# First chunk's weights and first x blocks packed by the host; T4's high part moved

## The chip, the cores and the metric

The kernel runs on one core of a Trainium2 chip. The metric is the device time of one execution in microseconds (us), as the median of several runs. A core has a matmul engine (PE, whose weight loads are listed apart as PEld), a vector engine (DVE), a scalar engine (ACT), GpSimd (POOL) and a sync engine (SP). Here SP issues all loads but a few, POOL issues the stores of intermediates, and 16 DMA engines carry them.

## The reference

An input x of 2048 rows (positions) by 512 columns goes through two branches, which a gate mixes. One branch is a Fourier mixing layer: real and imaginary products with 512 x 512 matrices, then with 2048 x 2048 matrices, real part only. The other is a gated feed-forward layer.

```python
a = x @ dft_hid_re.T
b = x @ dft_hid_im.T
y = dft_seq_re @ a - dft_seq_im @ b
h = silu(x @ w1) * (x @ w3)          # w1, w3: 512 x 1376
out = h @ w2                         # w2: 1376 x 512
g = sigmoid((x * gate_w).sum(-1, keepdims=True))
result = g * y + (1 - g) * out
```

All data are float32.

## The kernel before

Every float32 operand is split into a high part (a copy rounded to the type `F32R`, written by ACT: `high`, L108) and a low part (the source less its high part, a subtraction on DVE: `low`, L111). A product is three matmuls: high by high, and the two mixed ones (`mm3`, L119). One matmul has a 128 x 128 weight block and 512 moving columns.

On top of that, most products are done by a scheme of the Strassen kind: an operand is cut in a 2 x 2 arrangement of blocks, and seven products of sums of blocks replace eight. The blocks of x are called B11, B12, B21, B22, their sums T1 to T4 (`SUMS`, formed by `sum_xo`, L207, on DVE). The weights of w1 and w3 come in chunks of 128 columns; a chunk has four blocks, A11, A12, A22, A21, of 256 columns each, and sums of them (`sums_wb`, L246 to L249).

The program has an early stage, which makes silu(x w1) * (x w3) for all chunks and two groups of x (g = 0 and 1), and then a long stage of eight blocks for the sequence products and the product with w2. The change lies in the first forty microseconds of the early stage:

- Warm-up: DVE writes a bf16 tile of zeros, and `WARM` = 11 matmuls on it run while the first data come.
- Loads, all on the SP queue in the order in which they are written: A11 of chunk 0 (128 KB), B11 (512 KB), the other three blocks of chunk 0 (384 KB), B21, B12, B22 (512 KB each), then chunks 1 to 4 of the weights (512 KB each).
- Chunk 0 is done with the plain eight products: `half(i, j, w, x, start)` issues six matmuls into the bank C[i, j] (L428). The order is C00, C10 with B11, C00, C10 with B21, C01, C11 with B12, C01, C11 with B22. Each needs the splits that stand just before it in the program.
- Products of chunks 1 to 3 with B11 (`prod1`, bank X) and B21 (`prod2`, bank Y) follow, while ACT and DVE split the weights and make T1 to T4.
- From chunk 1 on, `gate_up(n)` does the other five products of a chunk, in the order X (T2), Z (T3), X of chunk n+3, X (T1), Z (T4), Y of chunk n+3, X (B22). Hooks named `early`, `second`, `mid` and `at_end` hold work of other parts that is to be written at set places in it. X is accumulated further after L373 has read it, and Z after ACT has copied it (L364).

The order on every engine is the written order (`manual_schedule`); an engine waits on semaphores for its operands. The places `F4` hold the raw x blocks: four of 512 KB, one for each block of the group, used again for the second group once the sums of the first are made. T2 is written over B11, T3 over B12 and T4 over B21.

Of the kernel before, what the change touches and what calls it, by code (L numbers as in the profile page):

```python
# [7 lines left out]
F32 = mybir.dt.float32  # L8
F32R = mybir.dt.float32r
# [3 lines left out]
P = 128  # L13
# [4 lines left out]
TB = 512  # L18
# [3 lines left out]
NG = NST // 2  # L22
NC = (F + P - 1) // P
NP2 = (NC + 1) // 2
WARM = 11
LOOK = 3
K = 9
W2_AT = (9, 11, 13, 15)
# [4 lines left out]
def fnet_swiglu_gate_kernel(  # L33
    ctx: ExitStack,
    tc: tile.TileContext,
    xn: bass.AP,
    xt: bass.AP,
    cc: bass.AP,
    dd: bass.AP,
    w13: bass.AP,  # L40
# [13 lines left out]
    nc = tc.nc  # L54

    def pool(name, bufs, side, space=None):
        kw = {} if space is None else {"space": space}
        cm = tc.tile_pool(name=name, bufs=bufs, side=side, reuse_waits="tile", **kw)
        return cm, cm.__enter__()
# [9 lines left out]
    xo0_cm, xo0 = pool("xo0", 1, "left")  # L69
    f4_a_cm, f4_a = pool("f4_a", 1, "right")  # L70
    wu_cm, wup = pool("wu", 1, "right")
    s1_cm, s1p = pool("s1", LOOK + 1, "right")
# [4 lines left out]
    xo1_cm, xo1 = pool("xo1", 1, "right")  # L77
# [18 lines left out]
    def wide(name):  # L96
        return take(F4, [P, 1024], F32, name)
# [9 lines left out]
    def high(hi, src):  # L107
        nc.scalar.activation(hi, src, AF.Copy)  # L108

    def low(hi, lo, src):  # L110
        nc.vector.tensor_sub(lo, src, hi.bitcast(F32))  # L111

    def split(hi, lo, src):
        high(hi, src)
        low(hi, lo, src)

    def mm3(ps, ah, al, bh, bl, first, last, chain=False):
        for n, (u, v) in enumerate(((ah, bh), (ah, bl), (al, bh))):
            nc.tensor.matmul(ps, u, v, start=first and n == 0, stop=last and n == 2,  # L119
                             skip_group_check=chain)  # L120
# [13 lines left out]
    def flat(ap):  # L134
        return ap.rearrange("p a n -> p (a n)")
# [53 lines left out]
    XO, ST = {}, {}  # L189
    XRAW = ("B12", "B11", "B21", "B22")  # L190

    def flat_x(ap):
        return ap.rearrange("p q n -> p (q n)")

    def load_xo(g, k):

        if g not in XO:
            XO[g] = (xo1 if g else xo0).tile([P, 2, 7, 2, 512], F32R, tag="xo", name=f"xo{g}")
        ST[g, k] = wide(f"xs{g}_{k}")
        nc.sync.dma_start(ST[g, k], xt[g, XRAW.index(k)])  # L200

    OPS = ("B11", "B21", "B22", "T1", "T2", "T3", "T4")
    SUMS = {"T1": ("B12", "B11"), "T2": ("B22", "T1"), "T3": ("B22", "B12"), "T4": ("B21", "T2")}

    def sum_xo(g, k, t):
        ST[g, k] = t
        nc.vector.tensor_sub(t, *(ST[g, v] for v in SUMS[k]))  # L207

    def xo_parts(g, k):
        o = XO[g][:, :, OPS.index(k)]  # L210
        return flat_x(o[:, 0]), flat_x(o[:, 1]), ST[g, k]

    def split_xo(g, k):
        split(*xo_parts(g, k))

    WS, WA, WB = {}, {}, {}

    def back(w):
        return w >= NC and SETS[w] > 0

    def load_w(w, lo=0, hi=4):
        if lo == 0:
            WS[w] = f4_a.tile([P, 4, 256], F32, tag=f"f4_{4 + w % (LOOK + 1)}", name=f"ws{w}")
        nc.sync.dma_start(WS[w][:, lo:hi].rearrange("p a n -> p (a n)"),
                          w13[SETS[w], :, lo * 256 : hi * 256])
# [7 lines left out]
    def wa_parts(w, lo, hi):  # L233
        return (*(flat(WA[w][:, h, lo:hi]) for h in range(2)), flat(WS[w][:, lo:hi]))

    def new_wa(w):

        WA[w] = wap.tile([P, 2, 3, 256], F32R, tag="wa", name=f"wa{w}")
# [24 lines left out]
    def prod(ps, n, wi, xi, start, chain=False):  # L263
        w = WSET[n]
        w, wi = (WA[w], wi) if wi < 3 else (WB[w], wi - 3)
        x = XO[ITEMS[n][1]]
        for q in range(2):
            sl = slice(q * P, (q + 1) * P)
            mm3(ps, w[:, 0, wi, sl], w[:, 1, wi, sl], x[:, 0, xi, q, :], x[:, 1, xi, q, :],
                start and q == 0, q == 1, chain)  # L270
# [51 lines left out]
    def store_h(n, k, h):  # L322

        c, g = ITEMS[n]
        j = min(c % (NP2 - 1) if c < NC - 1 else NP2 - 1, NP2 - 1)
        b = 2 * (NP2 - 1 <= c < NC - 1)
        nc.gpsimd.dma_start(hsp[g, b + k, j // 2, :, j % 2 * 512 : (j % 2 + 1) * 512], h)  # L327

    early, second, mid, at_end = {}, {}, {}, {}

    def run(work, n):
        for f in work.get(n, ()):
            f()

    def gate_up(n):
        last = NI - 1
        x, s1 = G.pop(n)
        z = bank(6 + n % 2, f"Z{n}")  # L340
        if n == last - 1:

            u2, g1 = (s1p.tile([P, 512], F32, tag="s1", name=f"{k}_{n}") for k in ("u2", "g1"))
        else:
            h = hp.tile([P, 1024], F32, tag="h", name=f"h{n}")
            u2, g1 = h[:, :512], h[:, 512:]
        u4 = u4p.tile([P, 512], F32, tag="u4", name=f"u4_{n}")
        nw = WSET[n + 1] if n < last else 0
        if nw in WB or nw == 0:
            nw = None  # L350
        elif back(nw):
            load_wb(nw)
            nw = None
        wa = WSET[n + LOOK + 1] if n + LOOK < last else 0
        if wa in WA or wa == 0:
            wa = None
        else:
            load_w(wa, 0, 3 if back(wa) else 4)

        prod(x, n, 4, 4, False, True)  # L360
        nc.scalar.activation(u2, x, AF.Copy)
        run(early, n)
        prod(z, n, 5, 5, True, True)
        nc.scalar.activation(u4, z, AF.Copy)  # L364
        run(second, n)
        if nw is not None:
            sums_wb(nw)
        if n + LOOK <= last:
            first1(n + LOOK)
        if nw is not None:  # L370
            high_wb(nw)
        prod(x, n, 3, 3, False, True)
        nc.vector.tensor_add(u4, u4, x)  # L373
        if nw is not None:
            low_wb(nw)
        run(mid, n)
        prod(z, n, 2, 6, False, True)
        nc.vector.tensor_add(u2, u2, z)
        nc.vector.tensor_mul(u2, s1, u2)  # L379
        store_h(n, 0, u2)  # L380
        if wa is not None:
            new_wa(wa)
            parts_a = wa_parts(wa, 0, 3)
            high(parts_a[0], parts_a[2])
        if n + LOOK <= last:
            first2(n + LOOK)
        if wa is not None:
            low(*parts_a)
        prod(x, n, 6, 2, False, True)
        nc.scalar.activation(g1, x, AF.Silu)  # L390
        put_score(n, 1, x)
        if n + LOOK <= last:
            gate1(n + LOOK)
        nc.vector.tensor_mul(g1, g1, u4)
        store_h(n, 1, g1)
        run(at_end, n)


    ctx.enter_context(tc.manual_schedule())
    load_w(0, 0, 1)  # L400
    load_xo(0, "B11")
    warm = s1p.tile([P, 1024], mybir.dt.bfloat16, tag="s1", name="warm")[:, :512]
    nc.vector.memset(warm, 0.0)  # L403
    wps = bank(7, "wps")
    for n in range(WARM):
        nc.tensor.matmul(wps, warm[:, :P], warm, start=True, stop=True)  # L406
    nc.scalar.activation(act0, warm[:, :24], AF.Silu)
    load_w(0, 1, 4)
    for k in ("B21", "B12", "B22"):
        load_xo(0, k)  # L410
    load_w(1)
    load_w(2)
# [4 lines left out]
    b12, a21 = zt[0].rearrange("p h a n -> p h (a n)"), zt[1][:, :, 0]  # L417
# [12 lines left out]

    def xo_half(k, q):
        i = OPS.index(k)
        return XO[0][:, 0, i, q], XO[0][:, 1, i, q], ST[0, k][:, q * 512 : (q + 1) * 512]

    s1 = s1p.tile([P, 512], F32, tag="s1", name="s1_0")
    g1 = u4p.tile([P, 512], F32, tag="u4", name="g1_0")
    h0 = hp.tile([P, 1024], F32, tag="h", name="h0")
    t1 = hp.tile([P, 1024], F32, tag="h", name="t1")
    new_wa(0)
    split(*wa_parts(0, 0, 1))  # L440

    hi, lo, src = xo_half("B11", 0)
    high(hi[:, :256], src[:, :256])
    nc.vector.tensor_copy(hi[:, 256:], src[:, 256:])
    low(hi, lo, src)
    split(*xo_half("B11", 1))
    half(0, 0, 0, 0, True)
    split(a21[:, 0], a21[:, 1], WS[0][:, 3])
    half(1, 0, None, 0, True)
    split(*wa_parts(0, 1, 3))  # L450
    for q in range(2):
        split(*xo_half("B21", q))
    half(0, 0, 1, 1, False)
    split(b12[:, 0], b12[:, 1], ST[0, "B12"])
    half(1, 0, 2, 1, False)
    split_xo(0, "B22")
    nc.scalar.activation(s1, C[0, 0], AF.Silu)
    half(0, 1, 0, None, True)
    WS.pop(0)
    load_w(4)  # L460
    sum_xo(0, "T1", t1)
    half(1, 1, None, None, True)
    nc.vector.tensor_mul(h0[:, :512], s1, C[1, 0])
    store_h(0, 0, h0[:, :512])
    sum_xo(0, "T2", ST[0, "B11"])
    half(0, 1, 1, 2, False)
    for w in (1, 2):
        new_wa(w)
        split(*wa_parts(w, 0, 3))
    half(1, 1, 2, 2, False)  # L470
    free(*zt)
    split_xo(0, "T2")
# [28 lines left out]
    def do(work, n, f, *a):  # L501
        work.setdefault(n, []).append(lambda: f(*a))


    do(early, 1, lambda: low(*xo_parts(0, "T1")))
    do(second, 1, lambda: split_xo(0, "T4"))
    do(second, 1, free, *(ST[0, b] for b in ("B11", "B21", "B12", "B22")))
    do(second, 1, sum_g, 2, y2)
    do(mid, 1, gate1, 2)
    do(early, 2, sum_g, 3, y3)  # L510
# [65 lines left out]
    for n in range(NI):  # L576
        if n in W2_AT:
            p = W2_AT.index(n)
# [4 lines left out]
        if n in A1_AT:  # L583
            p = A1_AT.index(n)
# [9 lines left out]
    n = NI - 1 - LOOK  # L594
# [332 lines left out]
    for i, (src, sp, p) in enumerate(late):  # L927
        blk, b = 1 + i // 2, i % 2
        n = (17, 24)[b]
# [11 lines left out]
    for p in range(KD):  # L941
        early = p < NG - NP2
# [71 lines left out]
```

## Time and profile before

| | before |
|---|---|
| median of 3 runs | 710.58 us (710.43 to 710.71) |
| profiled execution | 710.56 us |
| its span in the trace | 708.8 us |
| PE busy | 703.8 us (99%) |
| DVE busy | 605.4 us (85%) |
| ACT busy | 369.1 us (52%) |
| POOL busy | 64.0 us (9%) |
| HBM read, written | 114.82 MB, 57.16 MB |

The span runs from the first instruction of the program to the last. Busy time is the time in which an engine had an instruction in it; matmuls overlap one another in the pipeline, so the pace of PE is seen from the starts of groups of matmuls and not from their durations. In the timeline a row has the start, the duration, the engine, the line, the operation, the tiles (out <- in), the shape and a count, and in brackets the idle time before it and what ended it. A row with a count merges instructions that follow each other. PEclk is the granted PE clock.

### The profile page before, as it was taken

Reading aid. Unit: us, or ns where it says so; the run is one execution under the profiler, and the core shown is the slowest. Engines: PE = TensorE matmul, PEld = TensorE weight load, DVE = VectorE, ACT = ScalarE, POOL = GpSimd, SP = SyncE. Lnnn points to the kernel's source line nnn. Section 1 sums busy time; section 2 is a strip of 40 time slices with the busy share of each in tenths; the row PEclk is TensorE's granted clock in tenths of the full one; section 3 lists DMA queues with packets and bytes.
Section 4 is the critical chain, followed back from the end, with each engine's and each line's share of the span. In section 5 each row is a group of like instructions: output and inputs, shape, how many; then the busy total and the mean of one; then the engine's idle time right before and its main releaser. Section 6 shows DMA issues by size and latency. Waiting matters only on the chain.

```text
span 708.8 us, 8596 instructions
## 1 busy us (share of the span) xinstructions
PE 703.8 (99%) x3089; PEld 578.4 (82%) x3089; DVE 605.4 (85%) x735; ACT 369.1 (52%) x479; POOL 64.0 (9%) x118
## 2 busy tenths in 40 slices
PE   9999999999999999999999999999999999999997
PEld 6788888888888888888888888888888888888886
DVE  6989988787679999877999589969997896898985
ACT  6665555655446754454554553544455455455451
POOL 0021111221110000000110001100110000000000
PEclk9999999999999999999999999999999999999999
DMA  7575546499997566712596238914999971773932
GB/s 281 208 283 221 213 184 255 182 317 352 420 412 264 222 202 239 286 60 89 177 357 254 90 123 320 344 51 187 383 418 417 353 267 61 296 283 138 321 120 89
DMA packets 45403, 172.54 MB, mean 243 GB/s; under 512 B 5296, under 2 KB 5424, under 8 KB 41520
## 3 DMA queue, kind: packets, MB, share of 16 engines
q1 hardware_dynamic: 32464, 118.50, 45.5%
q0 software_dynamic: 12608, 52.97, 18.9%
q8 instruction: 24, 0.39, 0.2%
q10 hardware_dynamic: 288, 0.52, 0.2%
q14 instruction: 19, 0.16, 0.1%
HBM read 114.82 MB, written 57.16 MB: 243 GB/s over the span
## 4 chain that ended last, share of the span: by engine, by line
PE 99%; DVE 0%; issue 0%
PE P L119 69%; PE X L119 16%; PE Z L119 8%; PE Y L119 4%; PE C L428 2%; PE wps L406 1%; DVE zc L807 0%; DVE warm L403 0%
## 5 line engine op out<-in xcount | busy, mean ns | idle before, releaser
L119 PE MATMUL P<-zo,a 128*128 128x512 f32 x1344 | 305.5, 389 | 0.0
L119 PEld LDWEIGHTS P<-zo,a 128*128 128x128 f32 x1344 | 251.9, 188 | 53.4 <-DVE zo L111 1.1
L108 ACT ACTIVATE zo<-B 128x1024 fp32r<-128x1024 f32 (+1 forms) x182 | 189.2, 1045 | 184.5 <-PE P L119 95.2
L111 DVE TENSOR_TENSOR zo<-B,zo 128x1024 fp32r<-128x1024 f32 (+1 forms) x182 | 217.8, 1204 | 48.2 <-ACT zo L108 47.4
L119 PE MATMUL P<-zo,H 128*128 128x512 f32 x468 | 106.2, 389 | 0.0
L119 PEld LDWEIGHTS P<-zo,H 128*128 128x128 f32 x468 | 87.8, 188 | 18.2
L665 DVE TENSOR_TENSOR B<-B,B 128x1024 f32<-128x1024 f32 (+1 forms) x78 | 93.0, 1192 | 0.1
L119 PE MATMUL X<-xo,wb 128*128 128x512 f32 x378 | 92.8, 389 | 0.0
L119 PEld LDWEIGHTS X<-xo,wb 128*128 128x128 f32 x378 | 70.9, 188 | 15.0 <-DVE u L373 0.3
L119 PE MATMUL P<-zo,Y 128*128 128x512 f32 x336 | 76.3, 389 | 0.0
L119 PEld LDWEIGHTS P<-zo,Y 128*128 128x128 f32 x336 | 63.1, 188 | 13.1
L327 POOL DMA_DIRECT2D hsp<-h x42 | 23.0, 547 | 127.5 <-DVE h L379 75.5
L119 PE MATMUL Z<-xo,wa 128*128 128x512 f32 x126 | 32.3, 390 | 0.0
L119 PE MATMUL X<-xo,wa 128*128 128x512 f32 x126 | 32.0, 389 | 0.0
L119 PE MATMUL Z<-xo,wb 128*128 128x512 f32 x126 | 32.0, 389 | 0.0
L119 PE MATMUL Y<-xo,wa 128*128 128x512 f32 x126 | 32.0, 389 | 0.0
L668 DVE TENSOR_TENSOR B<-B,B 128x1024 f32<-128x1024 f32 x26 | 31.7, 1219 | 0.0
L882 ACT ACTIVATE zu<-P 128x512 f32<-128x512 f32 x32 | 19.1, 598 | 20.3 <-PE P L119 20.3
L119 PEld LDWEIGHTS Z<-xo,wa 128*128 128x128 f32 x126 | 23.6, 188 | 5.3 <-DVE xo L111 0.4
L119 PEld LDWEIGHTS Z<-xo,wb 128*128 128x128 f32 x126 | 23.6, 188 | 4.9
L119 PEld LDWEIGHTS X<-xo,wa 128*128 128x128 f32 x126 | 23.6, 188 | 4.9
L373 DVE TENSOR_TENSOR u<-u,X 128x512 f32<-128x512 f32 x21 | 14.4, 687 | 15.5 <-PE X L119 15.5
(135 smaller groups left out, 550.6 us busy)
## 6 DMA issues: line engine op xcount, KB each, us to landing
B<-cc SPq DMA_DIRECT2D x64, 512.0 KB, 6.2
hsp<-h POOLq DMA_DIRECT2D x42, 256.0 KB, 3.6
B<-hsp SPq DMA_DIRECT2D x20, 512.0 KB, 10.3
wbsp<-wb POOLq DMA_DIRECT2D x8, 1024.0 KB, 4.2
wb<-wbsp SPq DMA_DIRECT2D x8, 1024.0 KB, 7.9
B<-zsp SPq DMA_DIRECT2D x16, 512.0 KB, 8.3
H<-w2sp SPq DMA_DIRECT2D x6, 1024.0 KB, 8.8
ws<-w SPq DMA_DIRECT2D x11, 512.0 KB, 4.3
```

Of the source, the lines that this page charges most:

```text
L108: nc.scalar.activation(hi, src, AF.Copy)
L111: nc.vector.tensor_sub(lo, src, hi.bitcast(F32))
L119: nc.tensor.matmul(ps, u, v, start=first and n == 0, stop=last and n == 2, skip_group_check=chain)
L327: nc.gpsimd.dma_start(hsp[g, b + k, j // 2, :, j % 2 * 512 : (j % 2 + 1) * 512], h)
L373: nc.vector.tensor_add(u4, u4, x)
L406: nc.tensor.matmul(wps, warm[:, :P], warm, start=True, stop=True)
L428: nc.tensor.matmul(C[i, j], wp(u, sl), xp(r, v), start=start and r == n == 0, stop=not start and r == 1 and n == 2)
L665: nc.vector.tensor_add(t, t, RAW[blk, b, q][:, :n])
L668: nc.vector.tensor_sub(t, RAW[blk, "B12", q], t)
L882: nc.scalar.activation(U[name][:, r], ps[r], AF.Copy)
```

## The change

The host packs a new input, `first`, of four pieces with 128 rows of 768 columns (384 KB each). Each piece has one weight block of chunk 0 and half a block of x side by side: A11 with B11's first half, A21 with B11's second half, A12 with B21's first half, A22 with B21's second half. They are loaded in four transfers, ahead of B12 and B22, into a tile that lies where the second group's split x will be later. `ST` and `RAW0` point into that tile, so B11 and B21 are now read, summed and overwritten in two strided halves (`halves`).

The splits of chunk 0 follow the order of the pieces. All 512 columns of B11's first high half are copied by DVE (before: half by ACT, half by DVE), ahead of A11's split. The split of chunk 1 is written ahead of T2's sum, that of chunk 2 stays behind it.

The warm-up reads a constant of ones that the program's preamble makes, so the memset goes, and `WARM` is 8, not 11.

T4's split, in `gate_up(1)`, gets a hook of its own, `ahead`, in front of ACT's copy of Z; before, it was behind that copy.

The four places of `F4` are now needed for B12 and B22 alone, so two are free when the second group's loads are written.

```diff
-WARM = 11
+WARM = 8
...
+    def halves(ap):
+        return ap if len(ap.shape) == 3 else ap.rearrange("p (q n) -> p q n", q=2)
+
     def sum_xo(g, k, t):
         ST[g, k] = t
-        nc.vector.tensor_sub(t, *(ST[g, v] for v in SUMS[k]))
+        nc.vector.tensor_sub(halves(t), *(halves(ST[g, v]) for v in SUMS[k]))
...
         prod(z, n, 5, 5, True, True)
+        run(ahead, n)
         nc.scalar.activation(u4, z, AF.Copy)
         run(second, n)
...
-    load_w(0, 0, 1)
-    load_xo(0, "B11")
-    warm = s1p.tile([P, 1024], mybir.dt.bfloat16, tag="s1", name="warm")[:, :512]
-    nc.vector.memset(warm, 0.0)
+    tf = xo1.tile([P, 2, 7, 2, 512], F32, tag="xo", name="first")
+    tf = tf.rearrange("p h o q n -> p (h o q n)")[:, : 4 * 768].rearrange("p (i n) -> p i n", i=4)
+    XO[0] = xo0.tile([P, 2, 7, 2, 512], F32R, tag="xo", name="xo0")
+    for i in range(4):
+        nc.sync.dma_start(tf[:, i], first[i])
+    ST[0, "B11"], ST[0, "B21"] = tf[:, 0:2, 256:], tf[:, 2:4, 256:]
+    RAW0 = {k: tf[:, i, :256] for i, k in enumerate(("A11", "A21", "A12", "A22"))}
+    warm = nc.const_aps.tensor(1.0, [P, 512], mybir.dt.bfloat16)
...
-    load_w(0, 1, 4)
-    for k in ("B21", "B12", "B22"):
+    for k in ("B12", "B22"):
         load_xo(0, k)
...
-    split(*wa_parts(0, 0, 1))
+    w_parts = lambda i, k: (WA[0][:, 0, i], WA[0][:, 1, i], RAW0[k])

     hi, lo, src = xo_half("B11", 0)
-    high(hi[:, :256], src[:, :256])
-    nc.vector.tensor_copy(hi[:, 256:], src[:, 256:])
+    nc.vector.tensor_copy(hi, src)
+    split(*w_parts(0, "A11"))
     low(hi, lo, src)
     split(*xo_half("B11", 1))
     half(0, 0, 0, 0, True)
-    split(a21[:, 0], a21[:, 1], WS[0][:, 3])
+    split(a21[:, 0], a21[:, 1], RAW0["A21"])
     half(1, 0, None, 0, True)
-    split(*wa_parts(0, 1, 3))
-    for q in range(2):
-        split(*xo_half("B21", q))
+    split(*w_parts(1, "A12"))
+    split(*xo_half("B21", 0))
+    split(*xo_half("B21", 1))
+    split(*w_parts(2, "A22"))
     half(0, 0, 1, 1, False)
...
     store_h(0, 0, h0[:, :512])
+    new_wa(1)
+    split(*wa_parts(1, 0, 3))
     sum_xo(0, "T2", ST[0, "B11"])
     half(0, 1, 1, 2, False)
-    for w in (1, 2):
-        new_wa(w)
-        split(*wa_parts(w, 0, 3))
+    new_wa(2)
+    split(*wa_parts(2, 0, 3))
...
-    do(second, 1, lambda: split_xo(0, "T4"))
-    do(second, 1, free, *(ST[0, b] for b in ("B11", "B21", "B12", "B22")))
+    do(ahead, 1, lambda: split_xo(0, "T4"))
+    do(second, 1, free, *(ST[0, b] for b in ("B12", "B22")))
...
+    b11, b21 = (arrays["xt"][0, k].reshape(P, 2, TB) for k in (1, 2))
+    a11, a12, a22, a21 = arrays["w13"][0].reshape(P, 4, 2 * P).transpose(1, 0, 2)
+    arrays["first"] = np.stack([
+        np.concatenate(v, 1) for v in
+        ((a11, b11[:, 0]), (a21, b11[:, 1]), (a12, b21[:, 0]), (a22, b21[:, 1]))
+    ])
```

More of the change, by code (lines that the diff above doesn't have):

```diff
@@ L37, in fnet_swiglu_gate_kernel @@
     xt: bass.AP,
+    first: bass.AP,
     cc: bass.AP,
@@ L203, in fnet_swiglu_gate_kernel @@
     SUMS = {"T1": ("B12", "B11"), "T2": ("B22", "T1"), "T3": ("B22", "B12"), "T4": ("B21", "T2")}
+    def halves(ap):
+        return ap if len(ap.shape) == 3 else ap.rearrange("p (q n) -> p q n", q=2)
     def sum_xo(g, k, t):
         ST[g, k] = t
-        nc.vector.tensor_sub(t, *(ST[g, v] for v in SUMS[k]))
+        nc.vector.tensor_sub(halves(t), *(halves(ST[g, v]) for v in SUMS[k]))
     def xo_parts(g, k):
         o = XO[g][:, :, OPS.index(k)]
-        return flat_x(o[:, 0]), flat_x(o[:, 1]), ST[g, k]
+        return o[:, 0], o[:, 1], halves(ST[g, k])
     def split_xo(g, k):
@@ L327, in store_h @@
         nc.gpsimd.dma_start(hsp[g, b + k, j // 2, :, j % 2 * 512 : (j % 2 + 1) * 512], h)
-    early, second, mid, at_end = {}, {}, {}, {}
+    early, ahead, second, mid, at_end = {}, {}, {}, {}, {}
     def run(work, n):
@@ L432, in xo_half @@
         i = OPS.index(k)
-        return XO[0][:, 0, i, q], XO[0][:, 1, i, q], ST[0, k][:, q * 512 : (q + 1) * 512]
+        return XO[0][:, 0, i, q], XO[0][:, 1, i, q], halves(ST[0, k])[:, q]
     s1 = s1p.tile([P, 512], F32, tag="s1", name="s1_0")
@@ L458, in fnet_swiglu_gate_kernel @@
     half(0, 1, 0, None, True)
-    WS.pop(0)
     load_w(4)
@@ L996 @@
         "xt": np.stack(xq, 1).reshape(2, 4, P, 2 * TB),
+        "first": None,
         "cc": np.stack(cb, 1).reshape(NTB, 4, NG // 2, P, 2 * TB),
```

## The prediction

> **What bounds the kernel now.** I read the page first (busy shares, chain), then the timeline of the first 40 us, then the DMA issues. From the page:
>
> ```profile
> span 708.8 us, 8596 instructions
> PE 703.8 (99%) x3089; PEld 578.4 (82%) x3089; DVE 605.4 (85%) x735; ACT 369.1 (52%) x479; POOL 64.0 (9%) x118
> ...
> PE 99%; DVE 0%; issue 0%
> ```
>
> PE is the whole chain that ended last, from the first warm-up matmul on. So only two things can change the time: when the 3,078 real matmuls begin, and gaps between them. The change touches only the first 40 us; whatever it gains or loses there is carried unchanged to the end, because the rest is PE back to back. The PE rows of the timeline there (start, duration, line, tiles, count):
>
> ```profile
> 1.19 4.39 PE L406 MATMUL wps<-warm 128*128 128x512 bf16 x11 [1.19 <-DVE warm L403]
> ...
> 5.43 1.94 PE L428 MATMUL C<-xo,wa 128*128 128x512 f32 x6
> ...
> 7.21 1.53 PE L428 MATMUL C<-xo,a 128*128 128x512 f32 x6
> ...
> 8.57 3.00 PE L428 MATMUL C<-xo,wa 128*128 128x512 f32 x12
> ...
> 11.40 1.52 PE L428 MATMUL C<-b,wa 128*128 128x512 f32 x6
> 12.76 1.52 PE L428 MATMUL C<-b,a 128*128 128x512 f32 x6
> ...
> 22.28 1.52 PE L119 MATMUL X<-xo,wa 128*128 128x512 f32 x6
> ...
> 29.08 1.52 PE L119 MATMUL X<-xo,wb 128*128 128x512 f32 x6
> 30.44 1.82 PE L119 MATMUL Z<-xo,wa 128*128 128x512 f32 x6
> 32.10 1.52 PE L119 MATMUL Y<-xo,wa 128*128 128x512 f32 x6
> ```
>
> Undisturbed, six matmuls take 1.36 us from start to start (11.40 to 12.76), 0.227 each. By that measure the trace loses time at these places: 5.43 to 7.21 is 1.78, so 0.42 lost; 8.57 to 11.40 is 2.83 for twelve, 0.11 lost; 30.44 to 32.10 is 1.66, 0.30 lost. The row at 11.40 follows 24 real matmuls, so PE stands as if it had begun at 11.40 - 24 x 0.227 = 5.95 and never stopped. I call that the effective start; the first part of the change has to lower it. One more loss comes at the next rows of all engines:
>
> ```profile
> 32.77 0.68 DVE L373 TENSOR_TENSOR u<-u,X 128x512 f32<-128x512 f32 x1
> ...
> 33.50 3.05 PE L119 MATMUL X<-xo,wb 128*128 128x512 f32 x12
> ...
> 36.38 1.55 PE L119 MATMUL Z<-xo,wb 128*128 128x512 f32 x6
> ```
>
> PE takes 1.40 before the row at 33.50 and 2.88 for its twelve, 0.20 more than undisturbed, because L373's add ends only at 33.45. Waits after that are few and have nothing to do with the change.
>
> **Part 1, the first loads.** Before, a 128 KB transfer (A11) and a 512 KB one (B11) must land before the first real matmul. Issue rows (KB each, us from issue to landing), then the two issues and their first users:
>
> ```profile
> ws<-w SPq DMA_DIRECT2D x1, 128.0 KB, 2.4
> ```
> ```profile
> xs_B<-xt SPq DMA_DIRECT2D x1, 512.0 KB, 3.8
> ```
> ```profile
> 0.74 0.39 SPq L224 DMA_DIRECT2D ws<-w  x1
> 0.86 0.27 DVE L403 MEMSET warm<- 128x256 uint32 x1 [0.86 <-PEq L1004]
> 1.18 0.42 SPq L200 DMA_DIRECT2D xs_B<-xt  x1
> ...
> 3.60 0.42 DVE L111 TENSOR_TENSOR wa<-ws,wa 128x256 fp32r<-128x256 f32 x1 [2.47 <-ACT wa L108]
> ...
> 4.96 0.94 ACT L108 ACTIVATE xo<-xs_B 128x256 fp32r<-128x256 f32 x2 [1.39 <-DMA xs_B<-xt]
> 4.96 0.29 DVE L444 CAST xo<-xs_B 128x256 fp32r<-128x256 f32 x1 [0.93 <-DMA xs_B<-xt]
> ...
> 5.41 1.29 DVE L111 TENSOR_TENSOR xo<-xs_B,xo 128x512 fp32r<-128x512 f32 x2 [0.15 <-ACT xo L108]
> ```
>
> So they land at 3.14 and 4.96. The number of transfers ahead of B12 stays four and the bytes 1,536 KB; only what comes first changes. After, 384 KB from one issue at 0.74 hold all that the first three matmuls need. When do they land? At the early end, the 128 KB landing plus 256 KB at the rate of a full queue:
>
> ```profile
> 6.00:7.00 1.00, 1.00 (x5) 0.70 (x5) 0.96 (x3) 0.71 (x2) 0.00 (x0) 1.00 1.02 406
> ```
>
> (last figure, 406 GB/s): 256 KB take 0.65, so 3.79. At the late end, B11's landing, after 640 KB, less the same 0.65: 4.31. B11 took 1.82 beyond A11 where 406 GB/s would need 1.29: 0.53 are lost at the joint of the first two transfers, where the engines are taken (1.04) but little moves:
>
> ```profile
> 2.40:2.90 0.50, 0.50 (x3) 0.18 (x2) 0.00 (x0) 0.00 (x0) 0.00 (x0) 1.00 1.04 176
> ```
>
> Whether that joint moves behind the first 384 KB or disappears, no row tells. I take 3.95, nearer the early end because the first transfer has no joint ahead of it, and call it L. The next three follow 0.97 apart (384 KB at 406 GB/s), the second up to 0.53 later if the joint costs as now.
>
> What follows L, by durations of the rows: ACT's high of A11 0.42 (the 256 shape), DVE's copy of all 512 columns between 0.29 (no dearer than 256) and 0.56 (plus 0.27, the step from 0.42 for a 256 subtraction to 0.69 for 512); I take 0.43. First matmul at L + 0.47, like 4.96 to 5.43 now. The low of A11 has moved from the waiting time at 3.60 onto the path: it starts after its high, L + 0.47, and ends L + 0.89; the low of the first B11 half follows, to L + 1.50; the third matmul, which reads it, starts at L + 1.55. Now it is 1.2 after B11's landing, so 0.35 of the earlier landing is given back here. A wait costs PE about 0.11 beyond itself, so the sixth matmul is due at L + 2.35. It needs the second half's high (0.63) and low (0.69) after the second landing at L + 0.97, about L + 2.38. So the seventh starts at L + 2.6 to 2.7, and the effective start is that less 1.36: L + 1.3 = 5.25, 0.70 earlier. Bounds: L = 3.79 and no wait gives 5.03, a gain of 0.9; the joint in full before the second transfer gives L + 0.97 + 0.53 + 1.42 for the sixth and 5.65 in all, a gain of 0.3; L = 4.31 gives about 0.35. I take 0.65. Further on, A12, B21 and A22 land at L + 1.9 and 2.9 and have their lows before their matmuls at L + 4 and later; the 0.11 at 8.57 goes.
>
> [...]
>
> **Part 2, the warm-up.** The memset (0.27 of DVE) goes, and PE no longer waits for it; other engines' first work starts at 0.74 to 0.86, so I take 0.8. Between these rows the loads come 0.43 apart, and only the last is quicker (0.10, not 0.15):
>
> ```profile
> 2.02 0.15 PEld L406 LDWEIGHTS <-warm 128*128 128x128 bf16 x1 [0.28 <-issue]
> ...
> 4.58 0.15 PEld L406 LDWEIGHTS <-warm 128*128 128x128 bf16 x1 [0.28 <-issue]
> ...
> 4.99 0.10 PEld L406 LDWEIGHTS <-warm 128*128 128x128 bf16 x1 [0.26 <-issue]
> ```
>
> PE thus runs at half pace until about 4.95, 3.8 after its start at 1.19. Eight matmuls of 0.427 end at 4.2, 0.2 before the first real one at 4.42. Cost nothing, as long as the pace still doubles near 4.6 to 4.95 (see the last rival).
>
> **Part 3, DVE and ACT order from 11 to 29 us.**
>
> ```profile
> 11.25 1.23 DVE L111 TENSOR_TENSOR xo<-xs_B,xo 128x1024 fp32r<-128x1024 f32 x1
> ...
> 14.12 1.22 DVE L207 TENSOR_TENSOR xs_B<-xs_B,t 128x1024 f32<-128x1024 f32 x1
> ...
> 15.26 1.82 DVE L111 TENSOR_TENSOR wa<-ws,wa 128x768 fp32r<-128x768 f32 x2
> 15.37 1.07 ACT L108 ACTIVATE xo<-xs_B 128x1024 fp32r<-128x1024 f32 x1 [1.82 <-DVE xs_B L207]
> ...
> 20.80 0.95 DVE L111 TENSOR_TENSOR wa<-ws,wa 128x768 fp32r<-128x768 f32 x1
> ...
> 26.15 1.22 DVE L207 TENSOR_TENSOR xs_B<-xs_B,xs_B 128x1024 f32<-128x1024 f32 x1
> ...
> 27.29 1.22 DVE L111 TENSOR_TENSOR xo<-t,xo 128x1024 fp32r<-128x1024 f32 x1
> ...
> 27.98 0.60 ACT L364 ACTIVATE u<-Z 128x512 f32<-128x512 f32 x1 [0.82 <-PE Z L119]
> 28.48 1.05 ACT L108 ACTIVATE xo<-xs_B 128x1024 fp32r<-128x1024 f32 x1
> ...
> 29.56 1.23 DVE L111 TENSOR_TENSOR xo<-xs_B,xo 128x1024 fp32r<-128x1024 f32 x1 [1.05 <-ACT xo L108]
> ```
>
> From 11.25 to 28.5 DVE runs without a pause, so it must stay ahead of a PE that arrives 0.65 earlier. The split of chunk 1 now precedes T2's sum: T2's high on ACT (1.07) can start only after that sum, with one low (0.87 from start to start) beside it, not two; DVE idles some 0.3. Against that, B22 (whose low is the row at 11.25) lands earlier, as the same bytes come with fewer losses: by 0 to 0.7. The tightest reader is the low of chunk 3 (20.80 to 21.75), which the third matmul of the group at 22.28 needs, at 22.73 now and 22.1 after. With DVE between 0.4 earlier and 0.3 later it ends at 21.3 to 22.05: no stall, or one of 0.1 to 0.2. I count 0.
>
> T4: its high waits behind Z's copy (27.98, until 28.48), though T4's sum is done at 27.37. Ahead of the copy it runs 27.4 to 28.45; its low follows T1's low at 28.5 to 29.75 and the 1.05 of idle DVE goes. PE needs it at the second matmul after 30.44, less 0.65: 30.0. So the 0.30 goes. Z's copy moves 0.5 later; Z's next write is at 30.44, which hides it, and so long as that holds it costs 0. Behind it, DVE's queue to L373 comes forward by up to 1.05, so most of the 0.20 at 33.50 goes too; PE arrives 1 us earlier there, so I take 0.15. Next late would be L373 again.
>
> SP: the next group's x loads wait for T2's buffer now; two of their places are free from the start after, so they go out right behind chunk 5's weights and compete with those and a store of h, which nobody awaits for microseconds: 0.
>
> **Sum.** 0.65 + 0.30 + 0.15 = 1.1 off the profiled execution's 710.56 (span 708.8 and 1.76 around it): 709.45. That execution is 0.02 under the median of 710.58, which is no difference.
>
> **Rivals.**
> A, the forecast: 709.45, own range 709.0 to 709.85. Chance 0.50.
> B, the joint vanishes and the first 384 KB land at 3.7 or sooner: gains 0.95 + 0.30 + 0.20, so 709.1. For it: one transfer has no joint. Against: B11's own 0.53. Chance 0.20.
> C, the earlier data don't help: the joint comes before the second transfer (gain 0.3), and DVE, 0.3 late by T2's bubble, stalls PE 0.2 at chunk 3. The new order of T4 alone is left: 0.1 + 0.45, so 710.0. For it: no DVE pause from 11.25 on. Against: same bytes, fewer joints. Chance 0.16.
> D, slower: the PE's pace does not double in time. Eight matmuls give 3.4 us of work and then a gap, less than the 3.8 that the rows above show. If the count starts again with the first real matmul at 4.42, PE stays at 0.427 each until 8.2. From the third matmul at 5.5 that is 2.7 us, 6.3 matmuls instead of 11.9, a loss of 1.3: 710.75. [...] It decides as soon as the pace doubles later than about 7.9. Against: PE is busy most of the time through the gap. The granted clock doesn't tell; it is the 1.00 in the rows of 2.40 and of 6.00 alike. Chance 0.14.
>
> [...]
>
> **How the numbers follow.** 0.2% of 710.58 is 1.42 us, about what a measurement of this kernel can tell from no change: below 709.16 is faster. That is 0.15 of B's 0.20 and a quarter of A, 0.28. Above 712.0 lies a third of D, 0.05. The rest, 0.67, is within. The range 708.9 to 710.8 leaves out B's end and most of the later D, under 2 in 10.
>
> **What would show it.** The first real matmul near 4.4 and the group that now starts at 11.40 near 10.7 show part 1; if the latter is at 11.1 or more, C. The Z group after T4's low without a wait, and the twelve after it in 2.72, show part 3. Matmuls of the first groups 0.43 apart, with no wait named, show D. A DVE wait of the X group near 21.7 shows the bubble. I am wrong if the first transfer lands after 4.4, or if PE's gaps move to a place that I count at 0.

## The result and the profile after

The changed kernel takes 712.34 us (median of 14 runs, 711.15 to 713.61) against 710.74 (14 runs, 710.43 to 711.08): ratio 1.0023, 95% interval 1.0015 to 1.0030. It is slower by 1.6 us where 1.1 less was forecast, outside the range of 708.9 to 710.8, and its runs spread over 2.5 us instead of 0.7. The profiled execution took 711.42, one of the quicker ones.

The page of the changed kernel, its span and the chain that ended last:

```profile
span 709.7 us, 8589 instructions
...
PE 98%; DMA 1%; ACT 0%; SPq 0%; DVE 0%; issue 0%
PE P L120 69%; PE X L120 16%; PE Z L120 8%; PE Y L120 4%; PE C L439 1%; DMA first<-first 1%; SPq L412 0%; DVE zc L819 0%; ACT xo L109 0%; ACT wa L109 0%
```

The new pieces (`first`) now stand in the chain: PE waits for transfers in a way that the chain of the kernel before, all PE, did not show. The timeline of the changed kernel, PE's rows (start, duration, line, tiles, count):

```profile
0.78 3.57 PE L418 MATMUL wps<-const-bfloat16-1.0 128*128 128x512 bf16 x8 [0.78 <-PEq L1024]
4.37 2.63 PE L439 MATMUL C<-xo,wa 128*128 128x512 f32 x6
6.84 1.56 PE L439 MATMUL C<-xo,a 128*128 128x512 f32 x6
8.49 3.32 PE L439 MATMUL C<-xo,wa 128*128 128x512 f32 x12
11.65 1.67 PE L439 MATMUL C<-b,wa 128*128 128x512 f32 x6
...
29.52 1.64 PE L120 MATMUL X<-xo,wb 128*128 128x512 f32 x6
31.00 1.77 PE L120 MATMUL Z<-xo,wa 128*128 128x512 f32 x6
32.61 1.53 PE L120 MATMUL Y<-xo,wa 128*128 128x512 f32 x6
```

Real matmuls begin 1.06 earlier (4.37, not 5.43), but the group after 24 of them begins at 11.65, not 11.40. The effective start is 11.65 - 5.44 = 6.2, later than the 5.95 of before. The row of 6.84 follows six real matmuls, and by it the effective start is still 6.84 - 1.36 = 5.48, earlier than before; the loss comes behind it: 1.65 to the row of 8.49, not 1.36, and 3.16 for its twelve, not 2.72. At the Z group (31.00) the gap that T4's move was to close is still 0.25 (1.61 to the next row).

Where the early start goes, from the same timeline, ACT and DVE (each row's bracket says what it waited for):

```profile
3.80 0.42 ACT L109 ACTIVATE wa<-first 128x256 fp32r<-128x256 f32 x1 [1.55 <-DMA first<-first]
3.80 0.43 DVE L454 CAST xo<-first 128x512 fp32r<-128x512 f32 x1 [3.80 <-DMA first<-first]
...
5.09 0.63 ACT L109 ACTIVATE xo<-first 128x512 fp32r<-128x512 f32 x1 [0.88 <-DMA first<-first]
...
7.50 0.42 ACT L109 ACTIVATE wa<-first 128x256 fp32r<-128x256 f32 x1 [1.48 <-DMA first<-first]
...
9.75 1.06 ACT L109 ACTIVATE b<-xs_B 128x1024 fp32r<-128x1024 f32 x1 [0.34 <-DMA xs_B<-xt]
```

The first piece is there at 3.80, at the early end. But the second and the third piece follow 1.29 and 2.41 apart instead of 0.97. The third, at 7.50, is what the twelve matmuls wait for. B12 comes at 9.75, at least 0.9 later than before (there ACT took it up at 8.86 and did not have to wait for it), although as many bytes stand ahead of it. The windows of 4 to 6 us (last figures: share of the DMA engines taken, GB/s), first of the kernel before, then of the changed one:

```profile
4.00:5.00 1.00, 1.00 (x4) 0.32 (x3) 0.07 (x2) 0.04 (x1) 0.00 (x0) 1.00 1.03 369
5.00:6.00 1.00, 1.00 (x5) 0.38 (x3) 0.85 (x2) 0.90 (x2) 0.00 (x0) 1.00 0.99 382
```
```profile
4.00:5.00 1.00, 0.98 (x3) 0.47 (x2) 0.98 (x3) 0.22 (x1) 0.00 (x0) 1.00 1.04 249
5.00:6.00 1.00, 0.93 (x4) 0.41 (x3) 0.52 (x2) 0.91 (x2) 0.00 (x0) 1.00 0.73 224
```

The second place is at 28 us. ACT's row there, and the issue row of the store of h's second half (KB, us to landing), changed kernel first, then before:

```profile
28.49 0.60 ACT L366 ACTIVATE h<-X 128x512 f32<-128x512 f32 x1 [2.07 <-DMA hsp<-h]
28.99 1.05 ACT L109 ACTIVATE xo<-first 128x1024 fp32r<-128x1024 f32 x1
```
```profile
hsp<-h POOLq DMA_DIRECT2D x1, 256.0 KB, 6.6
```
```profile
hsp<-h POOLq DMA_DIRECT2D x1, 256.0 KB, 3.4
```

Chunk 1 writes its h into the buffer of chunk 0's h, so ACT's copy of X must wait until that store has landed. Before, the store is issued at 20.59 and lands 3.4 later, at 24.0, and the copy waits for X alone:

```profile
26.56 0.60 ACT L361 ACTIVATE h<-X 128x512 f32<-128x512 f32 x1 [1.32 <-PE X L119]
```

So 2.6 us were to spare. In the changed kernel the store is issued at 21.82 and lands at 28.4. Which packets moved in between (packets, MB, share of the engines; q0 has POOL's stores, q1 the loads of SP), before from 20.6 to 24.0, then after from 21.9 to 25.9:

```profile
q1 hardware_dynamic: 144, 0.52, 47.0%
q0 software_dynamic: 80, 0.26, 19.0%
```
```profile
q1 hardware_dynamic: 313, 1.15, 96.7%
```

Before, the store goes out beside one load of 512 KB, that of chunk 5's weights. Now two loads of the second group's x stand right behind that one, and for these 4 us no packet of the store moves. Why it gets no share of the engines, no row tells.

T4's high (28.99) stands behind that copy on ACT. So my theory after the result was: late pieces, then a late store; the rival was PE at half pace (0.427 us a matmul, as in the warm-up, where 0.227 is undisturbed), since 8 warm-up matmuls end before the data.

About half of the difference between the two profiled executions (0.9 of span) is in neither place. The last store of the result is issued only 0.43 later than before (before, then after):

```profile
705.80 0.34 ACTq L808 DMA_DIRECT2D out<-zc  x1
```
```profile
706.23 0.34 ACTq L820 DMA_DIRECT2D out<-zc  x1
```

From there to the end of the span it is 3.0 us before and 3.5 after. It is 3.0 also in the profiles of T4's move alone and of the rows 4096 bytes apart in device memory, and 3.4 to 3.5 in all others below. What decides it was not tested, so differences of up to 0.4 between the medians below may hold such a step.

### The profile page after: what moved, and what is told of

Same layout as the page of the kernel before. It is cut to its first block, busy times and chain, and to the rows that moved or that the text cites. A ratio compares the mean times of both kernels' runs of the same rounds, so it can differ in the third digit from the quotient of the medians.

```text
span 709.7 us, 8589 instructions
## 1 busy us (share of the span) xinstructions
PE 704.5 (99%) x3086; PEld 578.0 (81%) x3086; DVE 605.2 (85%) x735; ACT 368.2 (52%) x479; POOL 64.0 (9%) x118
## 4 chain that ended last, share of the span: by engine, by line
PE 98%; DMA 1%; ACT 0%; SPq 0%; DVE 0%; issue 0%
PE P L120 69%; PE X L120 16%; PE Z L120 8%; PE Y L120 4%; PE C L439 1%; DMA first<-first 1%; SPq L412 0%; DVE zc L819 0%; ACT xo L109 0%; ACT wa L109 0%
## 5 line engine op out<-in xcount | busy, mean ns | idle before, releaser
L120 PEld LDWEIGHTS Y<-xo,wa 128*128 128x128 f32 x126 | 23.7, 188 | 4.9
```

## The experiments

Times are medians; "before" was measured again beside each group, at 710.84, 710.74, 710.82 and 710.94. Ratios are to the kernel before, with their 95% intervals in brackets.

**T4's move alone.**

```diff
         prod(z, n, 5, 5, True, True)
+        run(ahead, n)
...
-    do(second, 1, lambda: split_xo(0, "T4"))
+    do(ahead, 1, lambda: split_xo(0, "T4"))
```

> The kernel before, with T4's split moved ahead of Z's copy and nothing else. If the loss comes from the packed transfers and what they delay (my theory after the result), the move alone gains: T4's low ends at about 29.7 us, the gap of 0.30 at the Z group near 30.4 goes and most of the 0.20 near 33.5, so 710.2 to 710.3, with a spread between runs as small as before. If the move itself hurts (Z's copy comes later), 710.7 or more.

710.13 (709.84 to 710.41), ratio 0.9988 (0.9979 to 0.9997). Its PE rows at the place:

```profile
29.18 1.52 PE L119 MATMUL X<-xo,wb 128*128 128x512 f32 x6
30.54 1.52 PE L119 MATMUL Z<-xo,wa 128*128 128x512 f32 x6
31.90 1.52 PE L119 MATMUL Y<-xo,wa 128*128 128x512 f32 x6
```

1.36 from row to row: both gaps are gone. The gain of 0.7 is more than the 0.45 that I counted, but the interval holds 0.45 too. So the loss is in the rest.

**Eleven warm-up matmuls in the changed kernel.**

```diff
-WARM = 8
+WARM = 11
```

> The changed kernel with 11 warm-up matmuls in place of 8, so PE has no idle stretch before the first real matmul. If PE's pace doubling too late is what makes the runs slow and spreads them over 2.5 us (clock theory), the median falls to about 711.3 and the spread to under 0.5. If the slow and uneven transfers do it (transfer theory), both stay: median about 712.3, spread over 1.5. The profile will show the first matmul near 5.1 and the groups from the second on where they are in the changed kernel.

712.71 (712.08 to 712.94), ratio 1.0025 (1.0015 to 1.0034): not better, so a late doubling of PE's pace does not set the median; the narrower spread was not expected by either theory. Its profiled execution (712.79) has the store at its worst of all profiles, and may show what a typical run pays:

```profile
29.77 0.60 ACT L366 ACTIVATE h<-X 128x512 f32<-128x512 f32 x1 [3.29 <-PE X L120]
```
```profile
28.22 1.52 PE L120 MATMUL X<-xo,wa 128*128 128x512 f32 x6
30.42 1.66 PE L120 MATMUL X<-xo,wb 128*128 128x512 f32 x6 [0.68 <-ACT h L366]
31.92 0.44 PE L120 MATMUL Z<-xo,wa 128*128 128x512 f32 x1
32.63 1.41 PE L120 MATMUL Z<-xo,wa 128*128 128x512 f32 x5 [0.27 <-DVE xo L112]
```
```profile
hsp<-h POOLq DMA_DIRECT2D x1, 256.0 KB, 7.8
```

The store took 7.8 us, ACT idled 3.29 before its copy (the bracket names the X group, which had ended at about 27; it is the store that was late), and PE, whose next X group accumulates on the bank that ACT copies, took 2.20 instead of 1.36; then T4's low was late as well.

**Packed rows 4096 bytes apart in device memory.**

```diff
-        nc.sync.dma_start(tf[:, i], first[i])
+        nc.sync.dma_start(tf[:, i], first[i, :, :768])
...
+    arrays["first"] = np.pad(arrays["first"], ((0, 0), (0, 0), (0, 256)))
```

> The changed kernel with the packed rows stored 4096 bytes apart in device memory instead of 3072 (1024 unused bytes after each row); the transfers move the same 384 KB each. If the dense 3072-byte layout is what makes single packets of the third and fourth transfer take 1 us and more, these packets are gone, the third piece lands near 6.0 instead of 7.5, and the time falls to 710.0 to 711.0. If the layout has nothing to do with it, 712.3 and the third piece after 7.

711.52 (710.89 to 712.93), ratio 1.0012 (1.0003 to 1.0021). The third piece landed at 7.7, so the layout is not what makes it late. The median is 0.8 lower all the same, with intervals that overlap. The profiled execution has the late store and the late pieces as the changed kernel does; its end, after the last store, is 0.4 to 0.5 shorter, which may be part of it.

**The x loads held back.**

```diff
+    do(second, 1, lambda: F4.extend([F4.pop(0), F4.pop(0)]))
```

> The changed kernel with the second group's x loads held to about 26 us, as long as in the kernel before, by giving B11 and B21 the places of B12 and B22 (which are still read) instead of the two free ones. If these early loads slow the store of chunk 0's h, for which ACT's copy of X waits 2.1 us at 28.5, that wait goes, T4's high starts up to 0.45 earlier and the gap at Z falls by 0.2 to 0.35: about 712.0. If the store is late for another reason, the wait stays and the time is that of the changed kernel, 712.3.

710.85 (710.29 to 712.12), ratio 0.9999 (0.9990 to 1.0007). The store landed in 3.3 us, and ACT no longer waited for it:

```profile
26.79 0.60 ACT L366 ACTIVATE h<-X 128x512 f32<-128x512 f32 x1 [0.60 <-PE X L120]
```

That is 1.5 of the 1.6 that the change lost, and the two intervals are apart; I had expected 0.3, going by the profiled execution, which had a mild case of it.

**Two extra loads in the kernel before, with T4's move.**

```diff
+    def dummy():
+        v = xo1.tile([P, 2, 7, 2, 512], F32, tag="xo", name="extra")
+        v = v.rearrange("p h o q n -> p (h o q n)")
+        for k in range(2):
+            nc.sync.dma_start(v[:, k * 1024 : (k + 1) * 1024], xt[1, k])
+
+    do(early, 1, dummy)
```

> The kernel before with T4's move alone (710.13), and with two more loads of 512 KB that nobody reads, issued right behind chunk 5's weights, where the changed kernel's early x loads stand. Store theory: the store of chunk 0's second half of h lands 6 us or more after its issue instead of 4 to 5.5, ACT's copy of X near 26.7 waits for its buffer, T4's high and PE's Z group come late, and the time rises to 711.0 to 712.0. If the early loads only hurt together with the late pieces, it stays at 710.1 to 710.3.

711.10 (710.44 to 712.17), ratio 1.0006 (0.9997 to 1.0015), 1.0 above T4's move alone (the intervals just touch), and a spread of 1.7 instead of 0.6. The store landed in 7.2 us, where it took 3.2 with T4's move alone. The loads alone, in a kernel whose first transfers are those of before, bring the wait:

```profile
27.66 0.60 ACT L361 ACTIVATE h<-X 128x512 f32<-128x512 f32 x1 [2.43 <-DMA hsp<-h]
```

**Third and fourth piece as one transfer** (with held loads).

```diff
-    for i in range(4):
+    for i in range(2):
         nc.sync.dma_start(tf[:, i], first[i])
+    nc.sync.dma_start(flat(tf[:, 2:4]), rest)
```

> The changed kernel with the held x loads, and with the third and fourth piece as one transfer of 768 KB (6144 bytes a row), so one joint fewer ahead of B12. If the loss sits at the joints between short transfers (joint theory: the slow packets stand where one transfer follows another early in the program), the joined piece lands at 7.2 to 7.6 instead of 8.2 to 8.5, B12 and B22 come 0.3 to 0.6 earlier than with four pieces, and the time falls from 710.85 to 710.3 to 710.5. If it sits in the new input or its place on the chip, B22 still lands at 10.8 to 11.1 and the time is 710.8 or more.

711.90 (710.08 to 713.81), ratio 1.0015 (1.0006 to 1.0024): worse. The joined piece landed at 8.9 in the profiled execution (713.81), where the joint theory expected 7.6 at the latest. So one joint fewer did not bring the data earlier, and the number of joints isn't shown to be the price. That execution also shows PE at half pace, in its PE rows and in the granted clock (third figure from the end) of a window behind them:

```profile
6.79 1.52 PE L441 MATMUL C<-xo,a 128*128 128x512 f32 x6
9.91 4.64 PE L441 MATMUL C<-xo,wa 128*128 128x512 f32 x12 [1.60 <-ACT xo L110]
14.35 1.82 PE L441 MATMUL C<-b,wa 128*128 128x512 f32 x6
```
```profile
12.00:13.00 1.00, 1.00 (x3) 0.79 (x3) 1.00 (x2) 1.00 (x3) 0.00 (x0) 0.50 1.03 422
```

The six from 6.79 last 1.52 in all, as undisturbed. After the wait of 1.60 before 9.91, the twelve matmuls take 4.44 from start to start, where the changed kernel's took 3.16, and the clock from 12 to 13 is 0.50: PE had fallen back to half pace. How much of the median's loss is this, one profile can't tell.

**Two queues** (with held loads).

```diff
-        nc.sync.dma_start(tf[:, i], first[i])
+        (nc.scalar if i % 2 else nc.sync).dma_start(tf[:, i], first[i])
```

> The changed kernel with the held x loads, and with the second and fourth piece issued by ACT's queue instead of SP's. If one queue hands out its descriptors too slowly for 384 KB transfers (queue theory), the third piece lands near 6.0 and the fourth near 7.0, and the time falls to about 710.3. If the joints cost the same whoever issues, or the two queues' transfers only mix, the first piece lands later (up to 4.6, as it shares the engines with the second) and the time is 710.8 to 711.2.

710.53, ratio 1.0005 (0.9996 to 1.0014), in two groups: six runs from 710.42 to 710.53 and five from 711.69 to 712.11. The windows of 4 to 6 us:

```profile
4.00:5.00 1.00, 0.23 (x1) 0.00 (x0) 0.22 (x1) 0.22 (x1) 0.00 (x0) 1.00 1.03 409
5.00:6.00 1.00, 0.65 (x2) 0.37 (x2) 0.98 (x3) 1.00 (x3) 0.00 (x0) 1.00 1.03 413
```

409 and 413 GB/s where one queue gave 249 and 224, with the same pieces. So neither the new input nor its place is slow by itself. Over all profiles, the mean of these two windows is 236 to 325 with the packed pieces on one queue (nine profiles) and 385 to 414 with two queues (four); the first loads of the kernel before, on one queue, give 369 to 383 (three). The start gains nothing here: with pieces on both queues at once, the first lands at 4.78, about 1 later than on one queue and beyond the 4.6 that the rival expected, and the effective start is 11.46 - 5.44 = 6.02. In the packet records of the changed kernel, ten packets of 3072 bytes that start between 4.0 and 5.7 take 0.6 to 1.5 us (the usual is 0.12); here none that starts between 3 and 12 takes over 0.4. What it is in one queue with these pieces, no row tells.

**Twelve warm-up matmuls with two queues.**

```diff
-WARM = 8
+WARM = 12
```

> The kernel with the second and fourth piece on ACT's queue, with 12 warm-up matmuls instead of 8. Its runs fell in two groups, 710.4 to 710.5 and 711.7 to 712.1. If the upper group is PE at half pace because it stands idle from 4.2 to 5.35 (clock theory), 12 matmuls fill that gap and all runs lie at 710.4 to 710.7. If the groups come from the transfers, both stay.

710.52, all 11 runs within 710.42 to 710.57. The upper group is gone, as the clock theory said.

**Pieces 4096 bytes apart on the chip** (held loads, one queue).

```diff
-[:, : 4 * 768].rearrange("p (i n) -> p i n", i=4)
+[:, : 4 * 1024].rearrange("p (i n) -> p i n", i=4)[:, :, :768]
```

> The changed kernel with the held x loads, and with the four pieces 4096 bytes apart in the on-chip tile instead of 3072. If the place of the writes on the chip makes the packets slow, the third piece lands near 6 and the time falls to about 710.3; if not, no change against 710.85.

710.68 (710.37 to 711.44), ratio 1.0000, against 0.9999 with held loads alone: no difference that these runs tell. The third piece landed at 6.4 in the one profile, earlier than expected of a piece that stays late; other executions with one queue had it from 6.6 to 7.7. The store of h took 5.4 us in this profile, though the x loads were held, and ACT waited 0.86 for it: early loads are not the only thing that makes it late.

**Chunk 1's split behind T2's sum again** (held loads).

```diff
-    new_wa(1)
-    split(*wa_parts(1, 0, 3))
     sum_xo(0, "T2", ST[0, "B11"])
     half(0, 1, 1, 2, False)
-    new_wa(2)
-    split(*wa_parts(2, 0, 3))
+    for w in (1, 2):
+        new_wa(w)
+        split(*wa_parts(w, 0, 3))
```

> The changed kernel with the held x loads, and with the split of chunk 1 again behind T2's sum as in the kernel before. If DVE's bubble in front of T2's low (0.3 by my count) reaches PE through T4's low at 30.8, the gap of 0.11 there goes and the time falls by 0.1 to 0.3, to 710.6; if the order serves a PE that waits for chunk 1 at 17, a wait appears there and the time is the same or up to 0.3 more.

710.53 (710.25 to 710.98), ratio 0.9996 (0.9988 to 1.0005), 0.3 under held loads alone: as expected, though the intervals overlap and 0.3 is no more than the step at the end of the span.

**T4 back behind Z's copy**, in that kernel.

```diff
-    do(ahead, 1, lambda: split_xo(0, "T4"))
+    do(second, 1, lambda: split_xo(0, "T4"))
```

> Packed pieces on one queue, held x loads, old order of chunk 1's split, and T4's split back behind Z's copy. Without the move the gap at the Z group and at the twelve after it should be back: 0.3 to 0.7 above the 710.53 with the move, 710.85 to 711.2. If the packed kernel has no use for the move, 710.5.

710.89 (710.32 to 711.93): 0.36 more. What is left here of the change is the packed pieces and the shorter warm-up, and the ratio is 1.0002 (0.9993 to 1.0011): together worth nothing that shows. In the profiled execution (710.54, one of the quicker ones) the third piece came at 6.67 and the effective start was 10.78 - 5.44 = 5.34, 0.6 earlier than before and close to the forecast; most of that went again at the end, where it has the longer 3.4 us behind the last store.

**Eleven warm-up matmuls with one queue** (held loads, old order).

```diff
-WARM = 8
+WARM = 11
```

> One queue, held x loads, old order of chunk 1's split (710.53, runs from 710.25 to 710.98), with 11 warm-up matmuls instead of 8. If PE at half pace after a late doubling still costs this kernel something in its slower runs, the median falls to 710.3 to 710.4 and the runs lie within 0.3. If its spread is the late pieces' alone, the median stays at 710.5, or rises by the 0.1 that the longer warm-up puts before the third matmul, and the spread stays at 0.7.

710.63 (710.19 to 710.84), ratio 0.9997 (0.9989 to 1.0006), against 710.53: a late doubling of the pace costs this kernel nothing that shows.

**Two queues, the first piece alone, 10 warm-up matmuls** (held loads, old order).

```diff
-WARM = 8
+WARM = 10
...
-    for i in range(4):
+    for i in (0, 2):
         nc.sync.dma_start(tf[:, i], first[i])
...
     nc.scalar.activation(act0, warm[:, :24], AF.Silu)
+    for i in (1, 3):
+        nc.scalar.dma_start(tf[:, i], first[i])
```

> Held x loads, old order of chunk 1's split, 10 warm-up matmuls, first and third piece on SP's queue, second and fourth on ACT's queue behind the load of its function table, so that the first piece is alone at first. Queue theory: the first piece lands at 3.7 to 3.9, the others by 5.3, 5.6 and 6.6, with no packet over 500 ns after 3 us; real matmuls begin at 4.4 to 4.9 and the effective start is 5.3 to 5.6, so 709.5 to 709.8, below both kernels and below T4's move alone. If two queues do not help, 710.3 to 710.6 as with one.

709.95 (709.90 to 710.31), ratio 0.9990 (0.9981 to 0.9998), below both kernels. The first piece was not alone: ACT issued its transfers only 0.06 after SP's first (0.74), though they are written behind the table load.

```profile
0.80 0.87 ACTq L421 DMA_DIRECT2D first<-first  x2
```

So the first piece came at 4.34, later than expected. The effective start, 11.02 - 5.44 = 5.58, is in the expected range, the time just above it; profiles with the four pieces on one queue had it from 5.34 to 6.34, so what two queues show is the rate and runs within 0.4 us, not an earlier start than one queue can have. Against one queue in the same order (710.53) it is 0.6 lower, beside T4's move alone 0.2, both with intervals that overlap.

**The same with 8 warm-up matmuls.**

```diff
-WARM = 10
+WARM = 8
```

> The two-queue kernel with ACT's transfers behind its table load (709.95, runs from 709.90 to 710.31), with 8 warm-up matmuls instead of 10. The third matmul waits for data until about 5.9 either way. Clock theory: with 8, PE stands idle from 4.2 to 4.8 and some runs fall into an upper group, 1.0 to 1.6 above the others, while the lower group stays at 709.9. If a gap of 0.6 is too short to matter, no run lies above 710.4.

Median 710.00, ratio 0.9997 (0.9988 to 1.0006): seven runs from 709.78 to 710.02, five from 711.40 to 712.61. The profiled execution (711.82) is of the upper group. Its PE rows, and after them those of the kernel with 10:

```profile
5.19 3.03 PE L441 MATMUL C<-xo,wa 128*128 128x512 f32 x6 [0.84 <-DVE xo L456]
8.02 2.19 PE L441 MATMUL C<-xo,a 128*128 128x512 f32 x6
10.04 2.88 PE L441 MATMUL C<-xo,wa 128*128 128x512 f32 x12
```
```profile
4.91 2.15 PE L441 MATMUL C<-xo,wa 128*128 128x512 f32 x6
6.90 1.55 PE L441 MATMUL C<-xo,a 128*128 128x512 f32 x6
8.29 2.89 PE L441 MATMUL C<-xo,wa 128*128 128x512 f32 x12
```

Six matmuls from 8.02 to 10.04 take 2.02, not 1.36, with no wait named: half pace for the first of them, until about 9.3.

## Why the prediction was wrong, step by step

- **Part 3, SP's early loads, counted at 0.** This is the step that failed most. I wrote that nobody awaits what they compete with for microseconds, and 2.6 us of margin were there: ACT's copy of X awaits the store of h, because the pool of h has two buffers, and the store landed at 24.0 for a copy at 26.56. What I missed is that the loads do not slow the store a little: no packet of it moved for 4 us, and it took 6.6 to 7.8 us instead of 3.4. Held loads take 1.5 off the changed kernel, extra loads put 1.0 on another. The prediction had named this as a sign of being wrong: gaps at a place that it counts at 0.
- **Part 1, "the next three follow 0.97 apart".** The first landing (3.80), DVE's copy (0.43), the first matmul (4.37; I said 4.42) and the third's wait were as worked out, and up to the seventh matmul the start was earlier by 0.47. The second piece came 0.32 late, within the 0.53 that I bounded for the joint. The third, which I had at L + 1.9, so 5.85, came at 7.50, and the twelve matmuls from 8.49 waited for it. Nothing in the sum allowed for that. So the gain of 0.65 was about 0 over many runs: packing and warm-up without the rest stand at a ratio of 1.0002. That it lies at the joints isn't shown, as one joint fewer did not help. The bound of 5.65 was also added up wrongly: 3.95 + 0.97 + 0.53 + 1.42 is 6.87 for the sixth matmul, and so 5.74 for the effective start. Rival C came nearest, with a loss between the transfers and DVE's bubble, but it put the loss before the second piece and still had a gain; the runs gave less than that.
- **Part 3, DVE's bubble.** The size was right:

```profile
15.87 1.22 DVE L211 TENSOR_TENSOR first<-xs_B,t 128x1024 f32<-128x1024 f32 x1
17.01 0.95 DVE L112 TENSOR_TENSOR wa<-ws,wa 128x768 fp32r<-128x768 f32 x1
18.22 1.23 DVE L112 TENSOR_TENSOR xo<-first,xo 128x1024 fp32r<-128x1024 f32 x1 [0.26 <-ACT xo L109]
```

  0.26 idle in the changed kernel. The price was not: I covered it with a B22 that lands earlier, and B22 landed 0.9 later (11.04, not 10.15). Taking the new order back gave 0.3.
- **Part 3, T4's move, 0.45.** Right in its mechanism, and in its size as far as the runs tell. Alone it gave 0.7, in the packed kernel 0.36; in the changed kernel it gave little, as T4's sum and ACT's copy of X were both late.
- **Part 2, the warm-up.** PE started at 0.78 and the eight end at 4.2, as said. A pace that doubles late, as rival D has it, shows with two queues, where an upper group lies 1.2 to 2.8 above the lower: in the one profile of that group (711.82) the six matmuls from 8.02 last 2.19, and take 2.02 to the next row, not 1.36. That puts the doubling at about 9.3, an estimate with 0.427 for a matmul at half pace and 0.227 undisturbed. In the profile of the changed kernel it is absent: the six from 6.84 last 1.56, as at full pace. The chances put a third of D above 712.0; by the same paces that takes a first doubling near 10.9, and no profile shows one so late. That a count starts again with the first real matmul was an assumption; what starts the doubling, no run shows. More warm-up matmuls helped neither the changed kernel nor the one with held loads and one queue. So D was not the cause of the median here, though the time went its way; its executions above 712 were not profiled. The first real matmul stands at 4.37 here and at 5.19 to 5.35 in the profiles with two queues and 8 warm-up matmuls, which may be the difference.

The steps from the changed kernel back to the one before are: early loads +1.5, split order +0.3, T4's move -0.36, the rest +0.1, together +1.5 against the measured +1.6. As each step starts where the one ahead of it ends, the sum must come out near the whole; only the first step is clear of the intervals. By how much each of the changed kernel's runs had a late store stays open, since only one was profiled.

## What to carry to other kernels

Before a transfer is set free to start earlier, ask of every transfer that it will run beside, stores too, who waits for its buffer to come free, and how many microseconds of margin its present landing leaves. Do not assume that the two will share the engines: here the one issued later moved nothing for 4 us. Bytes and rate gave the landing of the first transfer (3.79 worked out, 3.80 measured); for the third on the same queue they did not (5.85 worked out, 7.50 measured), so look at GB/s by window. Two queues kept the rate up here (409 and 413 GB/s from 4 to 6 us, where one gave 249 and 224), at the price of a first piece that landed later (4.78, not 3.80). With two queues, let warm-up work reach up to the first real matmul, as the 12 matmuls did that kept all 11 runs within 0.15 us; with 8, five of 11 ran 1.2 to 1.7 longer. And a median should be judged by its spread, since two of these kernels ran in two groups more than 1 us apart.

## What the runs showed of the hardware

- With four pieces of 384 KB on one queue, or two of them and one of 768 KB, the mean rate from 4 to 6 us was 236 to 325 GB/s in nine profiles; with the pieces spread over two queues it was 385 to 414 in four.
- With two queues and 8 warm-up matmuls 5 of 11 and 5 of 12 runs were 1.2 to 2.8 us longer than the others of the same kernel; with 12 and with 10, none of 11 each. The one longer execution that was profiled (711.82) has the doubling of the matmul pace late: six matmuls from 8.02 took 2.02, not 1.36, with no wait named. Why some executions have it and others do not, no run shows.
- In the run with the joined piece, PE went from full pace (six matmuls from 6.79 lasting 1.52) through a wait of 1.60 us and the shorter waits behind it to a granted clock of 0.50 from 12 to 13 us.
- A store of 256 KB landed in 3.1 to 3.5 us beside one 512 KB load in eleven profiles and in 5.4 in one, and took 6.6 to 7.8 us with three such loads issued next to it in four. In the changed kernel no packet of it moved from 21.9 to 25.9 us, while the loads' packets took 96.7% of the engines.
